# Attention and two gated blocks on one core: the values of two heads as one step, and 1/sum loaded into the output tile

## The chip, the core and the metric

The kernel runs on one core of a Trainium2 chip. The core has TensorE (PE: matmuls and transposes, results to PSUM), VectorE (DVE), ScalarE (ACT), GpSimd (POOL) and SyncE (SP), whose queue starts nearly all DMAs. Each engine works through its own list in order and waits for semaphores of the others. The metric is the device time of one execution in microseconds (us); lower is better.

## The reference, cut to what matters

```
# 4 batches, 8 heads, 576 positions, head width 64
scores = q @ k.T / 8
cum    = cumsum(max(s, 0));  bias = -(cum[:, None] - cum[None, :])
scores = where(causal, -1e9, scores + min(bias, 0))
attn   = exp(scores - max);  attn = attn / (sum(attn) + 1e-9)
x      = attn @ v                          # 4 x 576 x 512 over all heads
# block 1: h = gelu(x @ w_in); u, v = halves of h
#   v = layernorm(v) * g_ln; v_s = w_sg @ v + b_sg; x = x + (u * v_s) @ w_out
# block 2: h = relu(x @ w_in2); the same with its own weights, no g_ln, no residual
```

All operands are float32. Products of the two blocks are taken as three float32r products of high and low parts; those of the attention are plain float32.

## The kernel before, in words

The heads of a batch are taken in pairs; there are 16 pairs, four a batch. For a pair, `transposes` (L604) turns q and k of both heads by TensorE; head 0 then lies on partitions 0 to 63 and head 1 on 64 to 127. `scores(i)` (L620) makes block i of 64 or 128 query rows for both heads, each head on one half of TensorE's rows: a float32 product of q and k (L635), then a float32r product that adds the bias (L638). VectorE adds the mask, takes the row minimum of the negated scores and copies to SBUF (L643), ScalarE takes exp and the row sum (L649). `seg` (L705) turns the exponentials by TensorE in four groups a head (L711) and copies them to SBUF by `copy` (L169). `values` (L717) multiplies them with v for one head: 12 matmuls whose outputs are 64 partitions wide, so each uses half of TensorE's columns. By the table USE the lower half of the columns gets pieces of 768 moving columns and the upper half 896, in one PSUM bank. `finish` (L724) copies the two parts out into the head's 64 partitions of the pair's tile x.

`denominators` (L651) takes the reciprocals of the row sums on VectorE, transposes them and writes them to a scratch tensor in DRAM with four small DMAs; `spread` (L662) reads them back with two DMAs that repeat a row over 64 partitions into a tile rb. When a pair enters the first block, GpSimd multiplies x by rb (L315), and x is split into float32r parts.

A TensorE record of a float32 matmul counts twice in the profile, so a head's 12 value matmuls are 24 records.

What sets the order: every piece of work is a step with a name, a place on a scale of heads and the steps it must follow (`Plan`, L59); `emit` runs through them by place. The places come from tables of numbers (PAIR, HEAD, MOE, WEIGHT and others), and ENG says which engine (A, D, P) does a copy or subtraction in batch 0, in batch 1, later, and in block 2. From the emitted steps a scheduler fixes each engine's list. While the first batch's attention runs, the weights of block 1 are loaded and split (L192 to L198); from then on matmuls of the blocks stand between the attention's steps. After the last pair the rest of block 1 and block 2 follow; the rows of block 2's spatial matrix are loaded, turned by TensorE (L210) and split one after the other through one staging tile.

Six PSUM banks go round among scores, transposes and values; two serve the blocks. SP's queue issues in order, and a DMA whose wait is open holds those behind it.

## Time and profile before

| what | us |
| --- | --- |
| median of 3 runs | 680.57 (677.62 to 680.93) |
| the profiled execution | 679.22 |
| its span, first to last instruction | 677.4 |
| TensorE busy | 659.8 (97%), 4733 matmul records |
| VectorE, ScalarE, GpSimd busy | 374.5, 359.5, 237.4 |
| mean granted TensorE clock | 0.991 |
| share of the chain that ended last | PE 90%, DVE 4%, DMA 3% |

The profile shows one execution. "Busy" counts an instruction from start to end, and for TensorE the end is modelled and reaches beyond the start of the next matmul; so the distance from start to start tells more of what a matmul costs than its duration. A row of the timeline merges neighbours of one line: "x24" is 24 records, and the second number is the time from the first start to the last end.

### The profile page before, as it was taken

The page shows a single profiled execution, that of the slowest core. Times are in us where ns is not written, and L with a number is a line of the kernel's source. Part 1 is how long each engine was busy: PE and PEld are TensorE (multiplying, and loading weights), DVE is VectorE, ACT ScalarE, POOL GpSimd, SP SyncE. Part 2 cuts the span into 40 slices and gives each one's busy share as a digit, 9 for nine tenths or more (in the row PEclk, how much of TensorE's full clock was granted, in tenths as well). Part 3 has the DMA queues.
Part 4 walks back from the last instruction along what each step waited for, and adds up shares of the span by engine and source line. Part 5 has one row for each costly group of instructions (what it writes and reads, how often), then busy time and mean ns, then how long its engine had stood idle before and what let it go on. Part 6 is the DMA issues. An engine that isn't in the chain of part 4 may idle for free.

```text
span 677.4 us, 13008 instructions
## 1 busy us (share of the span) xinstructions
PE 659.8 (97%) x4733; PEld 577.4 (85%) x4733; DVE 374.5 (55%) x1060; ACT 359.5 (53%) x927; POOL 237.4 (35%) x340
## 2 busy tenths in 40 slices
PE   8999999999999999999999999996999999999997
PEld 5877786789888889897888989995998998998996
DVE  7789969953538765547673488556792112111010
ACT  5678788874537664537562355326544426424322
POOL 2125634511621201412311544656594228014121
PEclk9999899999999999999999999999899999999999
DMA  6566663332331441330311433455241000010011
GB/s 156 149 167 196 162 185 105 82 88 55 96 94 26 121 106 25 97 89 8 104 54 36 132 122 87 130 157 176 74 130 49 32 32 19 15 53 11 11 54 47
DMA packets 87193, 59.84 MB, mean 88 GB/s; under 512 B 64469, under 2 KB 72661, under 8 KB 87129
## 3 DMA queue, kind: packets, MB, share of 16 engines
q1 hardware_dynamic: 85928, 58.71, 30.6%
q8 instruction: 37, 0.61, 0.4%
q10 hardware_dynamic: 1200, 0.30, 0.2%
q14 instruction: 28, 0.22, 0.1%
HBM read 44.59 MB, written 14.39 MB: 87 GB/s over the span
## 4 chain that ended last, share of the span: by engine, by line
PE 90%; DVE 4%; DMA 3%; SPq 1%; issue 1%; ACT 0%; POOL 0%
PE acc L721 8%; PE pp L711 8%; PE s L635 6%; PE pm L418 3%; PE pm L420 3%; PE pm L419 3%; PE pb L445 3%; PE pb L444 3%; PE pb L446 3%; PE pm L339 3%; PE pm L444 2%; PE pb L418 2%; PE pb L339 2%; PE pb L340 2%; PE pb L420 2%; PE pb L419 2%
## 5 line engine op out<-in xcount | busy, mean ns | idle before, releaser
L649 ACT ACTIVATE p<-p,mx 128x576 f32<-128x576 f32 (+4 forms) x160 | 88.5, 554 | 27.7 <-DVE mx L643 27.1
L455 POOL TENSOR_TENSOR g<-u,g 128x256 fp32r<-128x256 f32 (+1 forms) x48 | 39.0, 816 | 163.3 <-ACT g L169 124.5
L635 PE MATMUL s<-qk 64*128 64x288 f32 (+4 forms) x384 | 72.0, 411 | 1.2 <-DVE qk L169 0.8
L643 DVE CUSTOM_DVE_ANT_0 p<-s,mask 128x448 f32<-128x448 f32 (+4 forms) x160 | 62.0, 422 | 15.4 <-PE s L638 14.9
L711 PE MATMUL pp<-idf,p 128*128 128x128 f32 x480 | 68.7, 277 | 1.1 <-DVE pt L169 0.9
L721 PE MATMUL acc<-pt,raw_v 128*64 128x64 f32 (+3 forms) x768 | 63.9, 290 | 1.3 <-DVE mx L643 1.3
L711 PEld LDWEIGHTS pp<-idf,p 128*128 128x128 f32 x480 | 53.6, 140 | 9.7 <-issue 1.9
L721 PEld LDWEIGHTS acc<-pt,raw_v 128*64 128x64 f32 x768 | 50.0, 139 | 12.8 <-issue 4.3
L638 PE MATMUL s<-bias,ones 64*64 64x64 f32 (+4 forms) x192 | 57.1, 467 | 0.0
L450 DVE TENSOR_TENSOR u<-u,pm 128x256 f32<-128x256 f32 (+1 forms) x32 | 14.3, 448 | 66.6 <-PE pm L449 66.5
L635 PEld LDWEIGHTS s<-qk 64*128 64x128 f32 (+1 forms) x384 | 36.9, 176 | 14.2 <-issue 6.0
L169 ACT COPY pt<-pp 128x512 f32<-128x512 f32 (+2 forms) x72 | 38.1, 542 | 18.0 <-PE pp L711 17.1
L370 POOL TENSOR_TENSOR sm<-sm,half_pow 128x1 f32<-128x1 f32 (+1 forms) x38 | 27.6, 728 | 45.6 <-DVE sm L369 41.3
L450 DVE TENSOR_TENSOR u<-u,pb 128x320 f32<-128x320 f32 (+1 forms) x32 | 14.6, 455 | 47.4 <-PE pb L449 47.4
L315 POOL TENSOR_TENSOR x<-x,rb 128x576 f32<-128x576 f32 x16 | 23.1, 1442 | 50.3 <-ACT x L169 46.1
L444 PE MATMUL pm<-sgh,vh 128*128 128x256 f32 (+1 forms) x128 | 39.0, 307 | 0.6 <-ACT sgh L216 0.6
L169 ACT CAST g<-u 128x256 fp32r<-128x256 f32 (+1 forms) x40 | 17.0, 434 | 42.1 <-DVE u L450 42.1
L291 POOL TENSOR_TENSOR xl<-x,xh 128x576 fp32r<-128x576 f32 x24 | 34.7, 1461 | 9.8 <-ACT xh L169 7.8
L444 PE MATMUL pb<-sgh,vh 128*128 128x320 f32 (+1 forms) x128 | 38.0, 297 | 0.0
L445 PE MATMUL pb<-sgl,vh 128*128 128x320 f32 (+1 forms) x128 | 38.0, 297 | 0.0
L445 PE MATMUL pm<-sgl,vh 128*128 128x256 f32 (+1 forms) x128 | 37.5, 294 | 0.2 <-DVE sgl L217 0.2
L418 PE MATMUL pm<-xh,inh 128*128 128x256 f32 (+1 forms) x120 | 37.2, 310 | 0.0
(258 smaller groups left out, 1989.0 us busy)
## 6 DMA issues: line engine op xcount, KB each, us to landing
rb<-rec_d SPq DMA_DIRECT2D x32, 144.0 KB
x_d<-x SPq DMA_DIRECT2D x16, 288.0 KB
x<-x_d SPq DMA_DIRECT2D x16, 288.0 KB
raw<-in_q_dram SPq DMA_DIRECT2D x32, 128.0 KB
raw_v<-in_v_dram SPq DMA_DIRECT2D x32, 128.0 KB
stage<-in_moe_w_in_dram SPq DMA_DIRECT2D x8, 512.0 KB
stage<-in_moe_w_in_dram SPq DMA_DIRECT2D x16, 256.0 KB
out_dram<-o SPq DMA_DIRECT2D x16, 256.0 KB
```

The costliest lines, as they stand in the source:

```text
L169: (e.copy if e is nc.scalar else e.tensor_copy)(out_, in_)
L291: engine("xlo", phase).tensor_tensor(xl[:, kk, :S], x, fl(xh[:, kk, :S]), ALU.subtract)
L418: nc.tensor.matmul(pu, W["inh"][:, kk, f], xh[:, kk, c], start=(kk == 0), stop=False)
L444: nc.tensor.matmul(pz, vh[sb][:, f], W["sgh"][:, sb, c], start=(sb == 0), stop=False)
L445: nc.tensor.matmul(pz, vh[sb][:, f], W["sgl"][:, sb, c], start=False, stop=False)
L455: engine("glo", phase).tensor_tensor(gl, u, fl(gh), ALU.subtract)
L635: nc.tensor.matmul(st[a, e][:m, c0:c0 + w], st["qk"][rows, 0, qc], st["qk"][rows, 1, kc], start=True, stop=False)
L638: nc.tensor.matmul(st[a, e][:m, c0:c0 + w], ones[rows, :m], bias[n % 2][rows, kc], start=False, stop=True)
L643: nc.vector.tensor_tensor_reduce(out=pts[g][i][:m, kc], in0=st[a, e][:m, c0:c0 + w], in1=mask[:m, d0:d0 + w], scale=-0.125, scalar=3e38 if ...
L649: nc.scalar.activation(p, p, AF.Exp, bias=mx[g][:m, i:i + 1], scale=-1.0, accum_out=sums[n % 2][:m, NB * e + i:NB * e + i + 1])
L711: nc.tensor.transpose(ps[:, w:w + 128], pt[qb][:, kb * 128:kb * 128 + 128], idr if qb == kb and kb else idf)
L721: nc.tensor.matmul(st["acc"][64 * a:64 * a + 64, a0:a0 + w], raw_v[m % 2][:, kb, odd], st["x"][i][:, c0:c0 + w], start=j in (0, 1), stop=j ...
```

## The change

- `values` is one step for a pair. It takes two PSUM banks; each entry of USE is done for head 0 on the lower half of the columns and straight after for head 1 on the upper half. So the two halves get equal pieces in turn, 1664 columns each, and both heads' turned exponentials are kept until then (a tile for each head and group).
- `spread` puts 1/sum into the pair's tile x itself. `finish` multiplies on VectorE, x = acc * x, in two instructions of 128 partitions (384 and 192 columns). The copies of `finish`, the tile rb and GpSimd's multiplication go. x is now taken at `spread`, which must follow the splitting of x three pairs before; before, `spread` followed the splitting of the pair before.
- Scores: the step S2 makes blocks 0 to 3 and S4 block 4; before, 0 to 2 and 3 to 4.
- Small DMAs: the reciprocals are written with one DMA in place of four, the two rows of bias come with one in place of two (the second part of a row now lies 32 partitions further on).
- Every place in the tables and several engines in ENG are new. Among these: the low part of block 1's input weights goes from GpSimd to VectorE, the normalisation of v in batch 0 from VectorE to GpSimd, the low part of x in batch 1 from GpSimd to VectorE, in block 2 the high part of the gated product from ScalarE to GpSimd.
- The attention's exponentials and a part of block 2's tiles are placed by hand in one stretch of SBUF. Paths that would transpose in float32r are added, but their limits RAW and QKW (32) are never reached by 16 pairs.

```diff
-            if layer == 1:
-                engine("xm", phase).tensor_tensor(x, x, pairs[b * KD + kk]["rb"], ALU.mult)
             split_x(x, st["xh"], st["xl"], kk, phase)
...
-            for e in range(2 if n else 0):
-                nc.sync.dma_start(out=fl(bias[n % 2][D * e:D * e + 2]), in_=cum_d[2 * n + e])
+            if n:
+                nc.sync.dma_start(out=fl(bias[n % 2][::32]), in_=cum_d[2 * n:2 * n + 2].rearrange("h i t -> (h i) t"))
...
-            for i in range(4):
-                nc.sync.dma_start(out=rec_d[n % 4][:, 32 * i:32 * i + 32], in_=rt[32 * i:32 * i + 2 * NB])
+            nc.sync.dma_start(out=rec_d[n % 4].rearrange("c (b i) -> b c i", b=4), in_=rt)
...
         def spread():
-            st["rb"] = rb = ap.tile([128, S], F32, tag="rb", name="rb")
+            x = x_of(b)(j)
             for e in range(2):
                 row = rec_d[n % 4][NB * e:NB * e + NB].rearrange("c p -> (c p)")[64:]
-                nc.sync.dma_start(out=rb[D * e:D * e + D], in_=row.rearrange("(o t) -> o t", o=1).to_broadcast([D, S]))
+                nc.sync.dma_start(out=x[D * e:D * e + D], in_=row.rearrange("(o t) -> o t", o=1).to_broadcast([D, S]))
...
-        plan.add(f"B{n}", t0 + head["B"], spread, [f"R{n}", f"sp1.{(n - 1) // KD}.{(n - 1) % KD}"])
+        plan.add(f"B{n}", t0 + head["B"], spread, [f"R{n}", f"sp1.{(n - XB) // KD}.{(n - XB) % KD}" if n >= XB else None])
...
         def values():
-            st["acc"] = psa.tile([128, 512], F32, tag="a", name="acc")
+            acc = pair["acc"] = [psa.tile([128, 512], F32, tag="a", name="acc") for i in range(2)]
 
             for j, (i, c0, w, kb, a, a0) in enumerate(USE):
-                nc.tensor.matmul(st["acc"][64 * a:64 * a + 64, a0:a0 + w], raw_v[m % 2][:, kb, odd], st["x"][i][:, c0:c0 + w],
-                                 start=j in (0, 1), stop=j in (9, 11))
+                for e in range(2):
+                    nc.tensor.matmul(acc[a][D * e:D * e + D, a0:a0 + w], raw_v[m % 2][:, kb, e], pair["x", e, i][:, c0:c0 + w],
+                                     start=j in (0, 1), stop=j in (9, 11))
 
         def finish():
-            x = x_t(h // 2)
-            copy("fc", phase, x[rows, :384], st["acc"][0:64, :384])
-            copy("fd", phase, x[rows, 384:], st["acc"][64:128, :192])
+            x, acc = x_t(h // 2), pair["acc"]
+            for a, c in enumerate((slice(0, 384), slice(384, S))):
+                nc.vector.tensor_tensor(x[:, c], acc[a][:, :c.stop - c.start], x[:, c], ALU.mult)
...
-WEIGHT = {"wv": (3.54, 0.99), "wu": (6.51, 1.82), "sg": (3.14, 5.74), "wo": (4.59, 6.75), "ahead": 0.88}
+WEIGHT = {"wv": (-0.99, 0.33), "wu": (6.32, 1.86), "sg": (2.65, 7.0), "wo": (-3.21, 6.28), "ahead": 3.45}
```

How the lists move at three places that the prediction speaks of. First TensorE's list of the kernel before, around the values of a late head (pp is a group of turned exponentials, pm a product of the blocks):

```order
1919 L711 MATMUL pp<-idf,p_1_147 128x128
1920 L711 MATMUL pp<-idf,p_2_149 128x128
1921 L721 MATMUL acc<-pt,raw_v_121 64x320 [waits DVE_49]
1922 L721 MATMUL acc<-pt,raw_v_121 64x192 x3
1923 L721 MATMUL acc<-pt,raw_v_121 64x64 x3
1924 L721 MATMUL acc<-pt,raw_v_121 64x192
1925 L721 MATMUL acc<-pt,raw_v_121 64x64 x2
1926 L721 MATMUL acc<-pt,raw_v_121 64x128
1927 L721 MATMUL acc<-pt,raw_v_121 64x64 [waits DMAHW7_49]
1928 L711 MATMUL pp<-idf,p_2_149 128x128 [waits DVE_49]
1929 L711 MATMUL pp<-idf,p_3_151 128x128 x2
1930 L711 MATMUL pp<-idf,p_4_153 128x128
```

TensorE's list of the changed kernel around the values of a pair:

```order
1431 L456 MATMUL pm<-r_212,s_115 128x256
1432 L748 MATMUL acc<-pt,raw_v_124 64x320 [waits DVE_49]
1433 L748 MATMUL acc<-pt,raw_v_124 64x320
1434 L748 MATMUL acc<-pt,raw_v_124 64x192 [waits DVE_49]
1435 L748 MATMUL acc<-pt,raw_v_124 64x192 x5
1436 L748 MATMUL acc<-pt,raw_v_124 64x64 x6
1437 L748 MATMUL acc<-pt,raw_v_124 64x192 x2
1438 L748 MATMUL acc<-pt,raw_v_124 64x64 x4
1439 L748 MATMUL acc<-pt,raw_v_124 64x128
1440 L748 MATMUL acc<-pt,raw_v_124 64x128 [waits DVE_49]
1441 L748 MATMUL acc<-pt,raw_v_124 64x64 x2
1442 L737 MATMUL pp<-idf,p_0_127 128x128 [waits Activation_49]
```

The 24 matmuls of a pair now stand together. Over the whole list the values stand in 47 unbroken pieces before and in 22 now, the scores in 44 before and 32 now, and TensorE turns into or out of a piece of values or scores 182 times before and 107 times now. Up to the first score of pair 7 these counts are 71 and 40 turns, and 22 and 9 pieces of values; up to there the changed list also has 48 block products of 256 columns and 13 transposes more.

Second, VectorE's list of the changed kernel at the finish of pair 7 (L754; xl is the low part of x, rows L301). Before there was no such place on VectorE in this batch: ScalarE copied, and GpSimd multiplied later:

```order
398 L179 COPY pt<-pp 128x384 [waits PE_49]
399 L301 TENSOR_TENSOR xl<-x,xh 128x576 [waits Pool_49]
400 L179 COPY pt<-pp 128x512 [waits PE_49]
401 L179 COPY pt<-pp 128x192 [waits PE_49]
402 L301 TENSOR_TENSOR xl<-x,xh 128x576 [waits Pool_49]
403 L475 TENSOR_TENSOR xr<-xr,pm 128x256 [waits DMAHW5_49,PE_49]
404 L475 TENSOR_TENSOR xr<-xr,pm 128x256 [waits DMAHW1_49,DMAHW2_49,DVE_49,PE_49]
405 L179 COPY pt<-pp 128x384 [waits PE_49]
406 L754 TENSOR_TENSOR x<-acc,x 128x384 [waits DMAHW3_49,DMAHW4_49,DMAHW0_49,DVE_49]
407 L754 TENSOR_TENSOR x<-acc,x 128x192
408 L301 TENSOR_TENSOR xl<-x,xh 128x576 [waits Pool_49]
409 L179 COPY qk<-pst 128x512 [waits PE_49]
```

Row 406 names DMAs and VectorE itself but not TensorE; so do the finishes of pairs 11 and 15, while the other 13 name TensorE too. Behind it stand the copies of the next pair's q and k.

Third, SP's list at the start, of the kernel before:

```order
1 L157 DMA sr<-in_s_dram 32x576
2 L588 DMA raw<-in_q_dram 128x4x64 x2
3 L589 DMA raw<-in_q_dram 64x2x64
4 L588 DMA raw_v_121<-in_v_dram 128x4x64
5 L588 DMA raw_v_121<-in_v_dram 128x4x64 [waits DMAHW0_49]
```

and of the changed one:

```order
1 L167 DMA sr<-in_s_dram 32x576
2 L194 DMA stage<-in_moe_w_out_dram 128x1024
3 L592 DMA raw<-in_q_dram 128x4x64 x2
4 L593 DMA raw<-in_q_dram 64x2x64
5 L194 DMA stage<-in_moe_w_in_dram 128x1024 [waits DMAHW0_49,DVE_49]
```

A 512 KB load of weights now stands ahead of the first q, a second behind it, and a third ahead of the second pair's q.

## Rows read from the trace of the kernel before

**Rows 1.** Windows: engines' busy time, start of pair 7 at 124.1 (clock, DMA last)
```profile
0.00:124.10 124.10, 117.78 (x900) 89.89 (x900) 102.46 (x313) 92.99 (x259) 46.86 (x81) 0.99 0.59 156
124.10:372.20 248.10, 248.10 (x2015) 217.24 (x2015) 148.32 (x481) 141.46 (x375) 59.30 (x74) 1.00 0.26 72
372.20:458.00 85.80, 85.29 (x568) 81.23 (x567) 57.10 (x125) 35.48 (x80) 44.83 (x64) 1.00 0.41 124
458.00:478.00 20.00, 13.75 (x67) 11.19 (x66) 14.54 (x37) 10.97 (x32) 11.85 (x20) 0.83 0.54 157
478.00:677.40 199.40, 194.87 (x1190) 177.88 (x1189) 52.11 (x106) 78.59 (x184) 74.54 (x105) 1.00 0.14 44
```

**Rows 2.** Windows of L721 (values) alone: PE, then weight loads
```profile
0.00:124.10 124.10, 26.66 (x288) 19.73 (x288) 0.99 0.59 156
124.10:372.20 248.10, 37.27 (x480) 30.30 (x480) 1.00 0.26 72
```

**Rows 3.** Timeline of PE around one whole head (start, length, line, what, records)
```profile
158.04 0.82 PE L711 MATMUL pp<-idf,p 128*128 128x128 f32 x6
158.70 1.04 PE L610 MATMUL pst<-idf,raw 128*128 128x128 f32 x8
...
163.12 0.71 PE L711 MATMUL pp<-idf,p 128*128 128x128 f32 x5
163.76 1.79 PE L721 MATMUL acc<-pt,raw_v 128*64 128x320 f32 x24
165.49 0.33 PE L711 MATMUL pp<-idf,p 128*128 128x128 f32 x1
```

**Rows 4.** Timeline of PE, values cut in pieces
```profile
55.10 0.75 PE L721 MATMUL acc<-pt,raw_v 128*64 128x320 f32 x2
55.78 0.77 PE L711 MATMUL pp<-idf,p 128*128 128x128 f32 x5
...
352.64 1.31 PE L721 MATMUL acc<-pt,raw_v 128*64 128x192 f32 x20
353.88 0.41 PE L418 MATMUL pm<-xh,inh 128*128 128x320 f32 x1
```

**Rows 5.** Timeline of PE, from block products into scores
```profile
174.90 0.28 PE L466 MATMUL pm<-g,outl 128*128 128x256 f32 x1
175.02 0.28 PE L464 MATMUL pm<-g,outh 128*128 128x256 f32 x1
175.23 1.55 PE L635 MATMUL s<-qk 64*128 64x448 f32 x7
```

**Rows 6.** Timeline of PE, spatial weights of block 2 (idle before, releaser, in brackets)
```profile
463.68 0.63 PE L210 MATMUL pb<-idf,stage 128*128 128x128 f32 x4 [1.68 <-DMA stage<-in_moe_w_spatial_dram]
...
468.38 0.66 PE L210 MATMUL pb<-idf,stage 128*128 128x128 f32 x4 [1.19 <-DMA stage<-in_moe_w_spatial_dram]
...
472.43 1.09 PE L210 MATMUL pb<-idf,stage 128*128 128x128 f32 x4 [2.57 <-DMA stage<-in_moe_w_spatial_dram]
...
474.81 0.63 PE L339 MATMUL pb<-inh,xh 128*128 128x512 f32 x1
...
478.31 0.39 PE L339 MATMUL pb<-inh,xh 128*128 128x512 f32 x1
```

**Rows 7.** Lines by form, DVE and POOL (busy, mean ns, idle before and releaser)
```profile
L169 DVE COPY x<-acc 64x384 f32<-64x384 f32 x24 | 13.1, 545 | 9.1 <-PE acc L721 8.2 <-POOL xl L291 0.7
L450 DVE TENSOR_TENSOR u<-u,pb 128x320 f32<-128x320 f32 x18 | 8.7, 483 | 28.2 <-PE pb L449 28.2
L315 POOL TENSOR_TENSOR x<-x,rb 128x576 f32<-128x576 f32 x16 | 23.1, 1442 | 50.3 <-ACT x L169 46.1 <-DMA rb<-rec_d 4.1
L397 DVE TENSOR_TENSOR vl<-g,vh 128x512 fp32r<-128x512 f32 x8 | 6.1, 756 | 6.8 <-ACT vh L169 6.7
```

**Rows 8.** Timeline of SP's queue, first reciprocals out and back
```profile
18.77 2.14 SPq L660 DMA_DIRECT2D rec_d<-rt  x4
22.44 1.12 SPq L666 DMA_DIRECT2D rb<-rec_d  x2
```

More of the change, by code (lines that the diff above doesn't have):

```diff
@@ L41 @@
[L41 to L52 removed]
+PA, PM, XB, RAW, LOW, QKW = 6, 2, 3, 32, 0, 32
@@ L391, in vc @@
                 if tb == NT:
-                    rest["v"] = w2p.tile([128, S + REM], F32R, tag="stg2", name="rest_v")[:, :DF]
                     v_parts(g[0:64], vh[NT], s14[0:64])
@@ L498, in keep @@
         def keep():
-            if first:
-                rest["g"] = w2p.tile([128, 8 * 128], F32R, tag="rest", name="rest").rearrange("p (i t) -> p i t", i=8)
             copy("rg", phase, rest["g"][:, :, 64 * (b % 2):64 * (b % 2) + 64], fl(st["g8"][:, :, 256:320]))
@@ L559, in attention_two_moe_kernel @@
         nc.gpsimd.memset(t, 1.0)
-    rec_d = [dr.tile([2 * NB, 128], F32, name=f"rec_d{i}") for i in range(4)]
+    rec_d = [dr.tile([32, 128], F32, name=f"rec_d{i}") for i in range(4)]
     ones = ap.tile([128, 128], F32R, name="ones")
@@ L566, in attention_two_moe_kernel @@
     for e in range(2):
-        nc.vector.memset(fl(ones[D * e:D * e + 2]), 1.0)
+        for i in range(2):
+            nc.vector.memset(fl(ones[D * e + 32 * i:D * e + 32 * i + 1]), 1.0)
     def cumulate():
@@ L594, in plan_pair, with fetch @@
         phase = min(b, 2)
+        words, qk_words = 2 * n >= RAW, int(2 * n >= QKW)
+        def fetch(r, queue=nc.sync):
+            r = r.rearrange("p (t e d) -> p t e d", t=2 * NT + 1, e=2)
+            for i, src in enumerate((q, k)):
+                load(r[:, NT * i:NT * i + NT], src, b, j, r[REM * i:REM * i + REM, 2 * NT], queue if i else nc.sync)
         def ldqk():
-            st["raw"] = ap.tile([128, (2 * NT + 1) * 2 * D], F32, tag="raw", name="raw")
-            r = st["raw"].rearrange("p (t e d) -> p t e d", t=2 * NT + 1, e=2)
-            for i, src in enumerate((q, k)):
-                load(r[:, NT * i:NT * i + NT], src, b, j, r[REM * i:REM * i + REM, 2 * NT], nc.scalar if n == 0 and i else nc.sync)
+            if qk_words:
+                nc.sync.dma_start(out=fl(raws[1]), in_=qk_d[n])
+            else:
+                fetch(raws[0], nc.sync if n else nc.scalar)
         def transposes():
-            raw = st["raw"]
+            raw, ident, like = raws[qk_words], idq if qk_words else idf, F32R if qk_words else F32
             c, cr = slice(0, NT * 128), slice(NT * 128, S)
@@ L708, in seg @@
             for qb, kb in SEG[i]:
-                nc.tensor.transpose(ps[:, w:w + 128], pt[qb][:, kb * 128:kb * 128 + 128],
-                                    idr if qb == kb and kb else idf)
+                pt, ident, turned, like = ((ptr[n % 3][qb], idq, idqr, F32R) if n >= RAW and qb >= LOW else
+                                           (pts[n % 3][qb], idf, idr, F32))
+                nc.tensor.transpose(ps[:, w:w + 128].bitcast(like), pt[:, kb * 128:kb * 128 + 128],
+                                    turned if qb == kb and kb else ident)
@@ L730, in plan_head @@
         step("X1", lambda: seg(1), [f"S4.{m}", f"X0.{n}", f"X1.{n - 1}"])
-        step("X2", lambda: seg(2), [f"X1.{n}", f"V3.{n - 1}"])
+        step("X2", lambda: seg(2), [f"X1.{n}"])
         step("X3", lambda: seg(3), [f"X2.{n}"])
-        step("V3", values, [f"X3.{n}", f"ldv{m}", f"V3.{n - 1}"])
-        step("F1", finish, [f"V3.{n}", f"F1.{n - 1}"] + x_free)
+        if odd:
+            where = HEAD0 if n < H else HEAD
+            plan.add(f"V3.{m}", n + where["V3"], values, [f"X3.{n - 1}", f"X3.{n}", f"ldv{m}"])
+            plan.add(f"F1.{m}", n + where["F1"], finish, [f"V3.{m}", f"F1.{m - 1}", f"B{m}"])
```

117 lines of the change are left out of this document (69 added, 48 removed).

## The prediction

> **What bounds the kernel now.** I read the windows first, cut at the first score of pair 7, at the end of the values, and around block 2's spatial weights; then the values alone, then TensorE's timeline at a few places.
>
> From 124.1 to 372.2 TensorE has no idle time at all, while VectorE is busy for 148.3 of 248.1 and ScalarE for 141.5 [rows 1]. What TensorE saves there is saved in the end, unless another engine makes it wait. From 478.0 on it is nearly as full, and the change does not touch its matmuls there. Up to 124.1 the picture is mixed: TensorE 117.8, VectorE 102.5, ScalarE 93.0 of 124.1, with DMA at 0.59 [rows 1]; TensorE's busy time is flattered by modelled ends, so this stretch is set by chains over three engines. From 458 to 478 TensorE is busy for only 13.75 of 20 [rows 1].
>
> **The values.** A whole head takes 1.73 from its first start to the next instruction's [rows 3]. A transpose inside a run takes 0.66 / 6 = 0.11, so the 0.64 before the values is five of them and 0.09 for turning from full width to half columns [rows 3]. Into scores the distance is 0.21 where it was 0.12 between block products, again 0.09 [rows 5]. I use 0.09 for every turn into or out of values and scores. That leaves 1.64 for a head's matmuls, in which the upper columns work off 896 moving columns and the lower only 768.
>
> After the change a pair brings 1664 columns to each half, in equal pieces. Scaled by the longer half, a pair takes 1.64 x 1664 / 896 = 3.05 in place of 3.28. After 124.1 there are 20 heads in 25 pieces (480 records, 37.27 busy [rows 2]). Each piece's busy time reaches 0.06 past the next start (1.79 against 1.73), so the pieces really take 37.27 - 25 x 0.06 = 35.8. Afterwards: 10 x 3.05 + 13 pieces x 0.09 = 31.7. Gain 4.1.
>
> Bounds. The rest of a cut head, 20 records with 704 columns on its longer half, takes 353.88 - 352.64 - 0.09 = 1.15, or 1.63 ns a column [rows 4]; by that a pair takes 2.72 and the gain is 35.8 - 28.4 = 7.4. If the halves only share one rate and balance gives nothing, a pair takes 3.28, and only fewer ends are saved: 35.8 - 34.0 = 1.8. I take 4.1, since it comes from the whole head, which is what the new step is made of.
>
> Here a rule speaks against the change. A cut piece of one 320-column matmul takes 0.68 - 0.09 = 0.59, with the other half empty [rows 4], so 1664 columns one after the other would take 3.07: the old step already runs at 1.87 times one half's speed. The Trainium skill's page "TensorE: Matmul & The Clock Gate", section on packing small matmuls, measures 2.38 times for three column tiles, 0.79 a tile; carried over to two tiles, my estimate is 1.6 times, which would leave nothing for balance. The trace is past that already, so I count it as a rival with a small chance: the lower bound 1.8, and the sum would be 2.3 less.
>
> **The turns.** After pair 7's start the lists show 111 turns before and 67 now; 12 of the 44 that go are ends of values, counted above. 32 x 0.09 = 2.9. It could be 0 where a turn hides under a wait, but TensorE has no idle time there [rows 1], and 4 if all 44 count.
>
> **Spatial weights of block 2.** Each load into the single staging tile can start only when TensorE has turned the one before; TensorE waits 1.68 + 1.19 + 2.57 = 5.4 for them [rows 6]. The clock then falls: a 512-column product shows 0.63 at 474.8 and 0.39 at 478.3 [rows 6], and the granted clock is 0.83 over these 20 us [rows 1], a third of them at the 1.2 GHz level, 3.4 lost at most, part of it while waiting anyway. I count 2.4. In the new list 48 residual products, then 36 of block 2's first product, then 13 and 12 products with a few others stand between one turn and the next. From load to load the old list takes 468.38 - 463.68 = 4.7 and 4.05 [rows 6]; the first two gaps are now 7 to 9 us and cover it, the last two about 3.7 to 3.9 and leave 0.5 to 1 each. So 1.5 of waiting stays and the clock holds: gain 5.4 - 1.5 + 2.4 = 6.3; bounds 0, if the load is late for another reason, and 8.8.
>
> **The first 124 us.** TensorE's own need falls: values from 26.66 - 22 x 0.06 = 25.3 [rows 2] to 6 x 3.05 + 9 x 0.09 = 19.1, and 31 turns go, 13 of them ends of values, so 18 x 0.09 = 1.6. Together 7.8. Into the room comes work from later, 48 block products at 0.12 [rows 5] and 13 transposes at 0.11, 7.2. If TensorE set the pace, pair 7 would begin at the same 124 and 7.2 would be missing later. VectorE hardly gets lighter up to there: 8 copies at 0.545 go [rows 7], with them 6 normalising steps and 4 casts, but 8 subtractions of 128x512 come, at 0.756 by the nearest row, and 12 multiplications; a 320-column multiplication from PSUM takes 0.483 [rows 7], so 384 and 192 columns are near 0.9 a pair. I put this at +1 us. The start is worse: 512 KB now stand ahead of the first q, at 156 GB/s [rows 1] 3.3 us, and some 1.2 MB more than before ahead of pair 1's, 8 us, though pair 0's turned exponentials and weight splitting can fill a part. I take a net gain of 4; bounds -4 (all 8 and 3.3 lost) and 10.
>
> **What costs nothing.** The copies out of the values leave ScalarE and the multiplication (23.1 us [rows 7]) leaves GpSimd; neither bounds. Fewer small DMAs: the four writes took 2.14 us of SP's queue for a pair, the two reads 1.12 [rows 8]; about 1.6 a pair is saved there, 26 in all, but TensorE never waited for these. It only brings 1/sum earlier. VectorE gets some 15 us more in the middle stretch (multiplications, subtractions); at 148 of 248 it has room, and if the cover fails it shows as waits for scores.
>
> **A wait is added.** finish now needs 1/sum on VectorE, with two of six PSUM banks held. Behind it stand the copies of the next groups and then the reductions of the scores, and TensorE waits for those. In the new list the values of a pair come after the scores of the next pair, some 20 us after its own, and the old round trip took 22.44 - 18.77 = 3.7 from writing to reading back [rows 8]. In 13 of 16 pairs the values come last; at pairs 7, 11 and 15 the DMA does. I count nothing.
>
> **Sum.** 4.1 + 2.9 + 6.3 + 4 = 17.3. The profiled execution took 679.2, 1.35 below the median of 680.57 and inside the three runs' spread. 679.2 - 17.3 = 662.
>
> **The rivals.**
> - Two halves at one rate (the rule above): values gain 1.8 in the middle and about 1 less at the start: 665.5. For it: nothing but the page; against: 1.87 already. 0.12.
> - The start slips and VectorE sets the first stretch: 4 becomes -4, 670. For it: VectorE's 102.5 of 124.1 and the loads ahead of q; against: TensorE was often what others waited for. 0.18.
> - The spatial loads stay late because SP's queue holds them behind other waits: 0 for 6.3, 668. For it: in-order issue; against: the first gaps of 7 to 9 us. 0.1.
> - Slower: finish waits for 1/sum. The place is VectorE's row of finish, worst where x comes free late. GpSimd once waited 4.1 for rb [rows 7]. If in each of the 12 pairs after the first batch VectorE stands for the round trip of 3.7 and the four free banks cover 1.7 of it, 12 x 2 = 24: 686. It decides from 17.3 / 12 = 1.4 a pair. For it: three finishes where the DMA is last; against: the 20 us ahead in the others. 0.08.
>
> **How the numbers follow.** My forecast has 0.52. The forecast's own bounds and the first three rivals lie from 649 to 675; below that needs every upper bound at once. About 0.5% (3.4 us) is what a measurement can tell from no change. Faster 0.88: the forecast and the three milder rivals, less a little for several of them together. Within 0.5%: 0.05, the milder ones added up. Slower: 0.07, nearly all of the last rival.
>
> **What would show it.** Right: values in at most 22 pieces, a whole pair near 3.1 from start to start; pair 7's first score near 124 with more block products before it; no wait of more than 1 us at the spatial transposes and a clock near 1.0 there; TensorE without idle time from there to the end of the values. Wrong: a pair's values at 3.4; a first score of pair 7 past 130; VectorE's finish idle on a DMA, with TensorE's transposes or scores waiting behind for copies.

## The result, and the profile after

The changed kernel takes 669.44 us (median of 4 runs, 667.86 to 669.82), the kernel before 680.63 in the same measurement; the ratio is 0.984, interval 0.981 to 0.987. The forecast was 662 with a range of 649 to 675: faster, as said, but by 11.2 us in place of 17.3. The profiled execution took 669.26, its span is 667.5.

The windows of the changed kernel, cut at the same events as [rows 1]: first score of pair 7 (now at 138.6), end of the values (363.8), 20 us around block 2's spatial weights, and the rest. Columns: window, length, busy time (records) of PE, PEld, DVE, ACT, POOL, then granted clock, DMA share, GB/s.

```profile
0.00:138.60 138.60, 124.06 (x962) 95.44 (x962) 102.70 (x329) 94.68 (x257) 47.33 (x90) 0.94 0.56 145
138.60:363.80 225.20, 225.17 (x1927) 197.66 (x1927) 153.31 (x493) 114.67 (x313) 35.77 (x56) 1.00 0.29 77
363.80:450.00 86.20, 84.42 (x577) 80.41 (x576) 56.87 (x129) 40.96 (x93) 36.54 (x46) 1.00 0.44 128
450.00:470.00 20.00, 18.91 (x105) 15.54 (x104) 15.18 (x37) 12.82 (x38) 10.04 (x20) 1.00 0.46 133
470.00:667.50 197.50, 192.51 (x1171) 175.75 (x1169) 55.04 (x122) 64.43 (x148) 75.16 (x122) 0.99 0.14 45
```

Two opposite things are to be seen. From pair 7's first score to the end it is 667.5 - 138.6 = 528.9 us, before it was 677.4 - 124.1 = 553.3: 24.4 less, of which 7.2 is work that now lies ahead of pair 7. So 17.2 are gained there, where the forecast had 4.1 + 2.9 + 6.3 = 13.3. Up to pair 7 it takes 14.5 us longer; 7.2 of that is the moved work, so 7.3 are lost where the forecast had a gain of 4. TensorE's own account of the 14.5: it is idle for 138.60 - 124.06 = 14.5 in place of 6.3 [rows 1], 8.2 more, and its mean granted clock up to pair 7 is 0.94 in place of 0.99, at most 0.06 x 138.6 - 0.01 x 124.1 = 7.1 more; its need at full clock would be about the same (forecast: 7.8 saved, 7.2 moved in).

The values alone, for the first two of these windows (to compare with [rows 2]), and the timeline of TensorE around two whole pairs (start, length, line, what, records):

```profile
0.00:138.60 138.60, 20.85 (x288) 16.59 (x288) 0.94 0.56 145
138.60:363.80 225.20, 31.35 (x480) 25.58 (x480) 1.00 0.29 77
```
```profile
244.34 2.98 PE L748 MATMUL acc<-pt,raw_v 128*64 128x320 f32 x48
247.25 1.64 PE L737 MATMUL pp<-idf,p 128*128 128x128 f32 x13
...
268.06 2.98 PE L748 MATMUL acc<-pt,raw_v 128*64 128x320 f32 x48
270.96 0.77 PE L737 MATMUL pp<-idf,p 128*128 128x128 f32 x5
```

A pair takes 2.91 and 2.90 from its start to the next instruction's; a single head took 1.73 [rows 3]. One count of columns has to be put right here: by the kernel's table USE, and by the records of the trace, a head has 768 moving columns on the lower half and 832 on the upper, not 896; a pair so brings 1600 columns to each half, not 1664.

The spatial weights of block 2, the same rows as [rows 6] (idle time before and its releaser in brackets):

```profile
447.96 0.65 PE L220 MATMUL pb<-idf,stg 128*128 128x128 f32 x4
...
456.89 0.60 PE L220 MATMUL pb<-idf,stg 128*128 128x128 f32 x4
...
461.55 0.66 PE L220 MATMUL pb<-idf,stg 128*128 128x128 f32 x4 [0.63 <-DMA stg<-in_moe_w_spatial_dram]
...
466.30 0.46 PE L220 MATMUL pb<-idf,stg 64*128 64x64 f32 x4
```

Waits of 5.4 have become 0.63 and 0.47 (the second at the fifth transpose of that row block), and the clock in these 20 us is 1.00 where it was 0.83.

Where the first stretch loses its time is seen in the starts of each pair's first score (from the timelines of TensorE; "other" counts TensorE's records in between that are neither scores, values nor transposes for the attention):

| from first score of | before, us | other | after, us | other |
| --- | --- | --- | --- | --- |
| start to pair 1 | 16.9 | | 26.3 | |
| pair 1 to pair 4 | 44.0 | 15 | 52.7 | 20 |
| pair 4 to pair 7 | 63.2 | 66 | 59.6 | 109 |

The first two lines lose 9.4 and 8.7; in the third the changed kernel does 43 records more in 3.6 us less. The start, in TensorE's timeline of the changed kernel, and four windows behind it:

```profile
1.17 4.88 PE L145 MATMUL idle<-first 128*128 128x512 bf16 x11 [1.17 <-DVE first L140]
8.10 1.06 PE L621 MATMUL pst<-idf,raw 128*128 128x128 f32 x8 [2.05 <-DMA raw<-in_q_dram]
...
10.04 2.38 PE L660 MATMUL s<-qk 64*64 64x64 f32 x12 [0.77 <-DVE qk L179]
```
```profile
10.00:12.50 2.50, 2.46 (x16) 1.90 (x17) 0.09 (x1) 0.00 (x0) 0.00 (x0) 0.51 1.10 274
...
17.50:20.00 2.50, 2.50 (x9) 1.73 (x6) 1.52 (x5) 1.74 (x6) 0.00 (x0) 0.50 0.16 36
...
22.50:25.00 2.50, 2.50 (x19) 2.50 (x19) 2.23 (x5) 2.50 (x6) 1.81 (x3) 0.76 0.57 129
25.00:27.50 2.50, 2.50 (x25) 2.16 (x24) 1.92 (x5) 1.69 (x5) 1.36 (x2) 1.00 0.50 110
```

TensorE waits 2.05 for q, which stands behind 512 KB of w_out, and 0.77 for a copy; behind these waits the granted clock is 0.50, the 1.2 GHz level, from 10 until about 23. Pair 0's scores and transposes take 16.3 us where they took 8.7. Then VectorE fills up; windows 30 to 60 of the kernel before and of the changed one:

```profile
30.00:40.00 10.00, 10.00 (x87) 8.06 (x85) 7.41 (x32) 8.24 (x28) 3.06 (x3) 1.00 0.56 153
40.00:50.00 10.00, 10.00 (x88) 8.20 (x87) 8.22 (x26) 7.01 (x22) 3.44 (x3) 1.00 0.64 161
50.00:60.00 10.00, 9.31 (x87) 7.18 (x86) 8.99 (x28) 9.02 (x23) 4.20 (x5) 1.00 0.66 183
```
```profile
30.00:40.00 10.00, 8.00 (x77) 5.81 (x76) 10.00 (x29) 6.43 (x16) 3.03 (x4) 1.00 0.58 159
40.00:50.00 10.00, 8.72 (x66) 6.54 (x64) 9.85 (x35) 7.01 (x21) 4.17 (x4) 1.00 0.77 221
50.00:60.00 10.00, 9.53 (x101) 8.00 (x102) 9.80 (x27) 8.20 (x23) 3.44 (x4) 1.00 0.75 176
```

Before, TensorE was full here and VectorE had room; now VectorE is full (29.65 of 30) and TensorE is idle for 3.75. The waits of TensorE, and those of VectorE for finish (us in total, times, longest):

```profile
PE pm L220 <- DMA stage<-in_moe_w_sg_dram: 2.3, 1, 2.3
PE pst L621 <- DMA raw<-in_q_dram: 2.0, 1, 2.0
PE pst L621 <- ACT pt L179: 1.6, 1, 1.6
PE pp L737 <- DVE mx L668: 1.5, 1, 1.5
...
PE pp L737 <- DVE x L754: 0.9, 3, 0.5
```
```profile
DVE x L754 <- DMA x<-rec_d: 4.8, 3, 2.6
...
DVE x L754 <- PE acc L748: 4.3, 4, 1.5
```

VectorE's finish does wait for 1/sum, 4.8 us in all, but only 0.9 of TensorE's waiting is put down to finish. The rival of a slower kernel did not come.

### The profile page after: what moved, and what is told of

The parts are those of the page before. It is cut to its first block, busy times and chain, and to the rows that moved or that the text cites. A ratio compares the mean times of both kernels' runs of the same rounds, so it can differ in the third digit from the quotient of the medians.

```text
span 667.5 us, 12894 instructions
## 1 busy us (share of the span) xinstructions
PE 645.1 (97%) x4733; PEld 564.8 (85%) x4733; DVE 383.1 (57%) x1109; ACT 327.6 (49%) x846; POOL 204.8 (31%) x332
## 4 chain that ended last, share of the span: by engine, by line
PE 81%; DVE 7%; DMA 6%; issue 2%; ACT 2%; SPq 1%; POOL 1%; DVEq 0%; POOLq 0%; ACTq 0%
PE pp L737 7%; PE s L660 7%; PE acc L748 6%; PE pm L347 3%; PE pm L425 3%; PE pm L348 3%; PE pm L427 3%; PE pm L426 2%; PE pm L451 2%; PE pb L453 2%; PE pb L452 2%; PE pb L451 2%; PE pm L453 2%; PE pm L452 2%; PE pb L427 2%
## 5 line engine op out<-in xcount | busy, mean ns | idle before, releaser
L668 DVE CUSTOM_DVE_ANT_0 p<-s,mask 64x64 f32<-64x64 f32 (+4 forms) x160 | 61.5, 422 | 13.1 <-PE s L663 12.6
L663 PE MATMUL s<-bias,ones 64*128 64x288 f32 (+3 forms) x192 | 53.8, 488 | 0.0
L748 PE MATMUL acc<-pt,raw_v 128*64 128x64 f32 (+3 forms) x768 | 52.2, 287 | 0.2
L748 PEld LDWEIGHTS acc<-pt,raw_v 128*64 128x64 f32 x768 | 42.2, 140 | 11.1 <-issue 2.5
L301 POOL TENSOR_TENSOR xl<-x,xh 128x576 fp32r<-128x576 f32 x20 | 28.8, 1457 | 69.2 <-ACT xh L179 69.0
L179 POOL CAST g<-u 128x256 fp32r<-128x256 f32 (+1 forms) x40 | 17.2, 441 | 106.6 <-DVE u L457 77.8
L179 DVE COPY pt<-pp 128x512 f32<-128x512 f32 (+1 forms) x72 | 37.2, 530 | 12.4 <-PE pp L737 11.8
L179 ACT COPY pt<-pp 128x512 f32<-128x512 f32 (+2 forms) x56 | 28.7, 532 | 31.1 <-PE pp L737 31.1
L497 ACT COPY o<-pb 128x512 f32<-128x512 f32 x13 | 7.5, 589 | 57.1 <-PE pb L495 55.1
L425 PE MATMUL pm<-xh,inh 128*128 128x320 f32 (+1 forms) x112 | 35.4, 316 | 0.0
L374 POOL TENSOR_SCALAR sm<-sm 128x1 f32<-128x1 f32 (+1 forms) x33 | 7.9, 240 | 87.7 <-DVE g L297 73.5
```

What stands on the lines that cost most here:

```text
L179: (e.copy if e is nc.scalar else e.tensor_copy)(out_, in_)
L301: engine("xlo", phase).tensor_tensor(xl[:, kk, :S], x, fl(xh[:, kk, :S]), ALU.subtract)
L425: nc.tensor.matmul(pu, W["inh"][:, kk, f], xh[:, kk, c], start=(kk == 0), stop=False)
L663: nc.tensor.matmul(st[a, e][:m, c0:c0 + w], ones[rows, :m], bias[n % 2][rows, kc], start=False, stop=True)
L668: nc.vector.tensor_tensor_reduce(out=pts[g][i][:m, kc], in0=st[a, e][:m, c0:c0 + w], in1=mask[:m, d0:d0 + w], scale=-0.125, scalar=3e38 if ...
L748: nc.tensor.matmul(acc[a][D * e:D * e + D, a0:a0 + w], raw_v[m % 2][:, kb, e], pair["x", e, i][:, c0:c0 + w], start=j in (0, 1), stop=j in ...
```

## The experiments

The question was the first stretch: forecast +4, found -7.3. Twelve kernels were run. "Pair 1", "pair 7" and "pair 8" are the starts of these pairs' first scores in the profiled execution; up to pair 7 all changed kernels have the same 140 TensorE records outside the attention (warm_longer has 7 warm-up products more), while up to pair 8 weights_as_before, bias_first and no_loads_good_start have 24 block products more than the others, worth 24 x 0.12 = 2.9. The ratio is taken to the kernel before in the same measurement (681.02 for the four rows from q_first, 678.80 from bias_first on, 679.98 from loads_gone on, 680.07 for the last), so compare rows by it. These starts are of one execution each, and executions of one kernel differ by several us.

| kernel | median | ratio to before (interval) | pair 1 | pair 7 | pair 8 |
| --- | --- | --- | --- | --- | --- |
| before | 680.63 | | 16.9 | 124.1 | 145.3 |
| changed | 669.44 | 0.984 (0.981 to 0.987) | 26.3 | 138.6 | 157.2 |
| q_first | 670.71 | 0.984 (0.980 to 0.988) | 28.3 | 141.2 | 159.8 |
| warm_longer | 665.91 | 0.979 (0.974 to 0.984) | 25.8 | 137.0 | 155.6 |
| weights_as_before | 670.51 | 0.985 (0.982 to 0.989) | 18.5 | 138.9 | 161.1 |
| values_by_head | 698.32 | 1.025 (1.022 to 1.029) | 25.4 | 143.0 | 164.1 |
| bias_first | 671.83 | 0.990 (0.987 to 0.994) | 23.3 | 140.2 | 162.5 |
| pair1_first | 667.38 | 0.982 (0.979 to 0.986) | 19.4 | 139.5 | 158.1 |
| spatial_as_before | 682.80 | 1.005 (1.002 to 1.008) | 26.6 | 139.8 | 158.4 |
| halves_unequal | 668.92 | 0.984 (0.981 to 0.988) | 25.3 | 132.9 | 151.7 |
| loads_gone | 667.48 | 0.983 (0.981 to 0.986) | 25.4 | 136.0 | 154.6 |
| before_loads_gone | 684.93 | 1.005 (1.003 to 1.008) | 19.4 | 127.0 | 146.2 |
| low_on_gpsimd | 667.68 | 0.983 (0.981 to 0.985) | 27.5 | 138.8 | 157.4 |
| no_loads_good_start | 663.79 | 0.978 (0.974 to 0.982) | 18.8 | 132.7 | 154.9 |

**q_first.**
```diff
-        plan.add(f"ldqk{n}", t0 + where["ldqk"], ldqk, [f"cp{n}", f"T{n - 1}"])
+        plan.add(f"ldqk{n}", t0 + where["ldqk"] - (20 if n == 0 else 0), ldqk, [f"cp{n}", f"T{n - 1}"])
```


> Edit: in the changed kernel the first pair's q is loaded ahead of the 512 KB of w_out instead of behind it; apart from a few neighbouring rows nothing moves. Theory (the first stretch lost its time at the start, where TensorE waits 2.05 us for q after its warm-up products and then runs at the 1.2 GHz level until about 20): the gap goes, the granted clock of the first 30 us is near that of the kernel before, pair 0's first score stands near 8.2 (10.0 in the changed kernel), pair 1's near 18 to 20 (26.3), pair 7's near 132 (138.6), and the time falls by 5 to 8 us to 661-664. Rival (the loads ahead of pair 1 and the splitting of weights on VectorE hold pair 1 back anyway): only the start moves, by some 2 us, pair 1 stays at 24 to 26, and the time is 667-669.

The gap before q is gone and pair 0's first score stands at 8.4, but the time is no better. The next wait took its place, the bias rows behind the same weights (TensorE's timeline):

```profile
8.40 1.34 PE L660 MATMUL s<-qk 64*64 64x64 f32 x12 [1.18 <-DVE qk L179]
13.06 1.11 PE L663 MATMUL s<-bias,ones 64*64 64x64 f32 x6 [3.32 <-DMA bias<-ch]
```

The clock fell as before (0.77 over the first 30 us in both). Both theories missed: pair 1 came later, not earlier.

**warm_longer.**
```diff
-MORE = {..., "w0": 11, ...}
+MORE = {..., "w0": 18, ...}
```


> Edit: 18 warm-up products instead of 11 on TensorE, about 3.1 us more at 0.44 us each, which cover the 2.05 us gap before q arrives; every load stays where the changed kernel has it. Theory that the clock alone costs it: pair 0's first score stays near 10, its scores take near 6 us instead of 10.7, pair 1's first score comes near 20 to 21 (26.3), the time falls by 4 to 6 us to 664-665. Rival (loads and splitting): pair 1 stays at 24 to 26 although the clock is up; time 668-670.

TensorE comes from the warm-up to q with little idle time, pair 0's first score stands at 9.3 with the clock up, and then waits 1.25 for the bias rows: by 12.5 the clock is down again, and pair 1 comes only 0.5 earlier. So this trace doesn't show a start with the clock up. The median lies near the expected time, but its interval overlaps that of the changed kernel. The six executions range from 663.0 to 672.5, and the time goes with the granted clock of the whole execution: 663.0 to 664.2 at 0.995 and 0.996, 667.6 to 672.5 at 0.979 to 0.989. The profiled one (667.6, 0.989) is of the second kind. This speaks for a price of the lower clock of some 5 us, without showing where in the kernel it is paid.

**weights_as_before.**
```diff
-WEIGHT = {"wv": (-0.99, 0.33), "wu": (6.32, 1.86), "sg": (2.65, 7.0), "wo": (-3.21, 6.28), "ahead": 3.45}
+WEIGHT = {"wv": (3.54, 0.99), "wu": (6.51, 1.82), "sg": (3.14, 5.74), "wo": (4.59, 6.75), "ahead": 0.88}
```


> Edit: the table of places for block 1's weights (loads and splitting) is that of the kernel before; all else as changed. Theory (the weights' places cost the first stretch 7 us more than the moved work explains): pair 1's first score near 18, pair 7's near 131, and the time falls by 5 to 8 us to 661-664. Rival C of the prediction (VectorE and the attention's steps set the first stretch, whatever the weights): pair 1 comes back to 18, but pair 7 stays at 136 to 139 and the time at 667-670, since VectorE is as full as before.

The start is healed: clock 1.00 over the first 30 us, pair 1 at 18.5. Yet pair 7 is at 138.9 and the time at 670.5. My theory failed; the times expected of rival C (the second rival of the prediction) came out to within 0.5 us. But its mechanism did not, as the windows from 30 to 100 show:

```profile
30.00:60.00 30.00, 25.76 (x202) 20.02 (x202) 23.43 (x78) 20.09 (x60) 6.44 (x8) 0.89 0.54 142
60.00:100.00 40.00, 33.56 (x269) 26.65 (x266) 32.87 (x98) 26.68 (x75) 12.59 (x15) 0.87 0.72 179
```

VectorE is not "as full as before": 23.43 of 30, where the changed kernel has 29.65. The chain of waits up to 139 now has 11.4% in loads of w_in and 6.6% in loads of w_sg: what no longer hinders the start comes late. And the lower clock has only moved: up to pair 7 the mean granted clock is 0.94, as in the changed kernel, and TensorE is idle for 17.4 in place of 14.5.

**bias_first and pair1_first.** The first loads of the weights are issued behind the bias rows (cum_d), or behind pair 1's q and k too:
```diff
+            def load_it(name=name, new=new, fetch=fetch, behind=layer == 1 and not before):
+                held[name] = new()
+                with tc.issue_after(last[-1].ins) if behind else nullcontext():
+                    fetch(held[name])
...
```


> Edit: the first loads of block 1's weights are issued on SP's queue behind the first pair's q and behind the bias rows (cum_d), instead of ahead of q; later loads keep their places. With q alone put first (q_first) TensorE waited 3.32 us for the bias rows behind the weights and the clock fell all the same. Theory: any of these waits at the start lets the clock fall to the 1.2 GHz level, and a start without them holds it: granted clock near 1.00 up to 30 us as in weights_as_before, pair 1's first score at 18 to 20, and as nothing else is moved, pair 7's near 131 to 133 and the time 661-665. Rival: the first 140 us are set by the chain of block 1's weights (load into the one staging tile, split on VectorE, next load), so pair 1 comes at 18 to 20 but pair 7 stays at 137 to 140, as in weights_as_before, and the time at 667-671.

> Edit: as bias_first, and the first weight loads stand behind pair 1's q and k as well, so they start some 3 us later still. Theory (the start decides): pair 1 is no earlier than in bias_first by more than 1 us, time within 2 us of bias_first. Rival (the chain of weights decides): the later the weights, the later pair 7: pair 7's first score 2 to 4 us behind bias_first's, time 2 to 4 us more.

In bias_first pair 1's k stands behind the weights (a wait of 2.9), pair 1 comes at 23.3; in pair1_first it comes at 19.4 and the clock is 1.00 over the first 30 us. In both, pair 7 stays at 140. So the theory that the start alone decides is refuted: moving pair 1 by 9 us moves neither pair 7 nor, beyond the intervals, the end. The rival was right on bias_first's pair 7 (not on its pair 1) and wrong on pair1_first: its later weights did not make pair 7 later. But pair1_first, too, is no kernel without the lower clock, which falls from 30 on (0.95 over the stretch up to pair 7):

```profile
30.00:60.00 30.00, 25.40 (x204) 19.40 (x201) 26.45 (x75) 19.06 (x56) 9.34 (x11) 0.93 0.70 194
60.00:100.00 40.00, 33.28 (x265) 28.11 (x263) 29.95 (x87) 24.81 (x68) 9.58 (x13) 0.88 0.53 153
```

**loads_gone and before_loads_gone.**
```diff
-        nc.sync.dma_start(out=st[:, 0:2 * n].bitcast(I32), in_=src.bitcast(I32))
+        if n < DF:
+            nc.sync.dma_start(out=st[:, 0:2 * n].bitcast(I32), in_=src.bitcast(I32))
...
+            raw = g_b.bitcast(I32).rearrange("p (n t) -> p n t", t=2)
...
```


> Left out: the 12 loads of 512 KB of block 1's w_in and w_out; every splitting step stays, but reads a tile of 256 KB that is loaded once at the start, so block 1 computes with other weights. Five starts have now given pair 1's first score anywhere from 18.5 to 28.3 and pair 7's always at 137 to 141. Theory W (the first stretch of the changed kernel is set by the weights' chain: load into a staging tile, 4 to 6.6 us each on the chain of waits, split, next load): without the loads pair 7's first score comes at 128 to 132 and the time falls by 6 to 10 us to 659-663. Rival V (VectorE's order sets it: 103 us busy of 138.6, with the splits, the copies and the scores' reductions in one list): the loads only filled time in which VectorE had other work; pair 7 at 135 to 139, time 666-669.

> Left out: the same 12 loads, in the kernel before. Theory W: there TensorE was idle for 6.3 of its first 124.1 us and loads stood on the chain for few us, so the kernel before gains less than the changed one: pair 7's first score at 120 to 123, time 675-679 (2 to 5 us less). Had both kernels the same cost from the loads (then they explain nothing of the missed gain): 8 to 10 us less, 670-672.

Without the 12 loads the changed kernel's pair 7 starts 2.6 earlier and its median is 2 us lower, within the intervals. The kernel before gains nothing, its median is 4.9 above that of the kernel before in the same measurement, outside both expectations. Its q now stands behind the 256 KB: pair 1 comes 2.5 later; pair 7 comes at 127.0, with 12 block products more ahead of it (1.4). Its twelve executions range from 678.5 to 686.2, and the profiled one took 679.1, so its trace does not show what made most of them longer. Theory W, that the loads alone set the first stretch, falls; alone they cost 2 to 3 us.

**low_on_gpsimd.**
```diff
-ENG = {..., "wlo": "DPPP", ...}
+ENG = {..., "wlo": "PPPP", ...}
```


> Edit: one letter of ENG; the low parts of block 1's w_in (8 subtractions of 128x512, 0.6 to 0.7 us each on VectorE in the changed kernel) go back to GpSimd, where they stood before and take about twice as long. Rival V (VectorE sets the first stretch): 8 x 0.65 = 5 us less for VectorE, time falls by 3 to 5 us to 664-666. Theory W (the chain of the weights): each split takes longer on the chain, time unchanged or up to 4 us more, 669-673.

VectorE loses 8 subtractions of 0.76, GpSimd gets them at 1.33. Pair 7 doesn't move (138.8), the time is 1.8 lower with overlapping intervals. So these eight subtractions are not, alone, what holds pair 7 back. Whether VectorE's fullness does is not settled: from 30 to 60 it is still busy for 28.5 of 30, and the clock up to pair 7 was lower in this execution (0.91 in place of 0.94).

**no_loads_good_start.** loads_gone, with the one 256 KB load behind the first two pairs' q and k:
```diff
+    def load_g():
+        with tc.issue_after(mark[0].ins):
+            nc.sync.dma_start(out=g_b, in_=moe_g_ln.rearrange("(o d) -> o d", o=1).to_broadcast([128, DF]))
...
```


> Left out: the loads of block 1's weights, as in loads_gone; and the one 256 KB tile that stands for them is loaded behind the first two pairs' q and k, so that neither q nor the bias rows have a large load ahead of them (in loads_gone TensorE still waited 1.1 us for q and ran at the lower clock to about 25). So far the start alone (pair1_first: pair 1 at 19.4, pair 7 at 139.5) and the loads alone (loads_gone: 25.4 and 136.0) each left pair 7 where it was. Theory T, a trade: either the attention starts late or the weights come late, and each alone is enough to hold pair 7 back: with both gone pair 1 comes at 18 to 20, pair 7 at 127 to 131, the time at 658-662. Rival O: what is left is the order of the attention's own steps in the first batch (scores, values of two heads, copies), which takes 18 to 19 us a pair whatever the weights do: pair 7 at 134 to 138 with an early pair 1 too, the time at 664-668.

Pair 1 comes at 18.8 and pair 7 at 132.7, 5.9 before the changed kernel's, with the same work ahead of it. (Pair 8 stands at 154.9, as in loads_gone, but with 24 block products more ahead of it.) The median is 663.8, the lowest of all, 5.6 below the changed kernel; the two intervals still overlap by 0.001. Both marks lie between theory T and rival O: with neither loads nor a late start 5.6 of the 7.3 us come back, and each pair still takes 16 to 24 us from there on. The lower clock is not gone here either (0.96 up to pair 7).

**values_by_head.**
```diff
-            for j, (i, c0, w, kb, a, a0) in enumerate(USE):
-                for e in range(2):
+            for e in range(2):
+                for j, (i, c0, w, kb, a, a0) in enumerate(USE):
```


> Edit: the values of a pair are issued head by head, 12 matmuls for the lower half of the columns and then 12 for the upper half, instead of in turn. The same matmuls, only their order differs. Theory (the two column halves run side by side only while pieces for both stand in turn; one half alone takes 0.59 us for 320 columns, 1.84 ns a column): a pair takes up to 2 x 1664 x 1.84 ns = 6.1 us instead of 2.9, less what overlaps at the change of heads; 16 pairs give +45 to +51 us, 714-720. Rival (both halves share one rate, so order doesn't matter and the gain of the step came from fewer turns alone): a pair stays near 2.9 to 3.0 and the time within 1% of 669.

```profile
173.80 5.44 PE L748 MATMUL acc<-pt,raw_v 128*64 128x320 f32 x48
179.17 0.77 PE L737 MATMUL pp<-idf,p 128*128 128x128 f32 x5
```

The same matmuls in another order take 5.37 a pair in place of 2.91: the two halves of the columns run side by side only while pieces for both stand in turn. The rival of one shared rate is refuted; the theory's 6.1 a pair and 714 to 720 were too high. The time rises by 29, less than 16 x 2.46 = 39, and the markers show where the rest is: from pair 7 to the end it is 552.5 in place of 528.9, 23.6 for ten pairs (24.6 expected), but pair 7's start moves only from 138.6 to 143.0, though six pairs bring 14.8 us more of TensorE's time. That is the clearest row of the study on the first stretch: some 10 us of TensorE's work there cost nothing, and the medians say the same (28.9 more, of which the ten later pairs account for 24.6). TensorE's idle time up to pair 7 is 10.4 in place of 14.5: part of the added work filled gaps.

**halves_unequal.**
```diff
+            for e in range(2):
+                for j, (i, c0, w, kb, a, a0) in enumerate(USE):
+                    nc.tensor.matmul(acc[e][D * a:D * a + D, a0:a0 + w], raw_v[m % 2][:, kb, e], pair["x", e, i][:, c0:c0 + w],
```


> Edit: the values stay one step for a pair, but each head goes to both column halves again, 896 columns on one half and 768 on the other, head 0 into one bank and head 1 into the other; finish takes four instructions of 192 columns instead of two, and multiplies the parts by 1/sum in the wrong places. Theory (the halves run side by side, each at its own pace, so the longer one sets the time): a pair takes 3.2 to 3.3 us instead of 2.93, 16 pairs 4 to 6 us, time 673-676. Rival (both halves share one rate): a pair stays at 2.9 to 3.0, time 669-671.

```profile
239.40 3.22 PE L748 MATMUL acc<-pt,raw_v 128*64 128x320 f32 x48
242.55 1.64 PE L737 MATMUL pp<-idf,p 128*128 128x128 f32 x13
```

A pair takes 3.15 where the changed kernel takes 2.91, so equal pieces in turn are worth 0.24 a pair; two heads apart took 2 x 1.73 = 3.46 [rows 3], so joining them in one piece is worth 0.31, of which 0.09 is one turn. The forecast for balance, 3.28 - 3.05 = 0.23, agrees by luck: with 832 and 1600 columns its sum gives 1.64 x 1600 / 832 = 3.15 in place of 3.05, and 0.13. The longer half's columns do not explain the rest; that pieces of unequal width stand in turn may, which no run separates. In the total nothing is seen: after pair 7 it is 529.9 against 528.9, and the first stretch of this execution happened to be 5.7 shorter, which no step of the edit explains; its six runs spread from 664.6 to 670.4, and the profiled one is the shortest. So one execution's pair 7 can move by as much as most of the differences in the table.

**spatial_as_before.**
```diff
-WEIGHT2 = {"wv": (-0.12, 5.87), "wu": (10.83, 13.19), "sg": (10.11, 10.44), "wo": (3.64, 1.59), "ahead": 4.44}
+WEIGHT2 = {"wv": (-0.17, 10.7), "wu": (11.01, 8.53), "sg": (14.19, 10.73), "wo": (-2.14, 3.37), "ahead": 4.88}
```


> Edit: the table of places for block 2's weights is that of the kernel before, so its spatial rows are turned by TensorE with 13, 21, 29 and 13 lines of the list between them instead of 47, 37, 16 and 18. Theory (TensorE waits for these loads, 5.4 us in the kernel before, and then runs at the lower clock): waits of 1 to 2.6 us come back at the two or three short gaps, the granted clock there falls below 0.95, and the time rises by 4 to 8 us to 673-677. Rival D of the prediction turned round (where the rows stand decides nothing, the loads are late or early for another reason): waits as in the changed kernel, 1.1 us together, time 668-671.

The old places cost 13.4 us by the medians, 14 by the ratios: the whole gain of the change and more, and more than the 4 to 8 expected. Windows of this kernel, and of the changed one:

```profile
440.00:460.00 20.00, 17.05 (x86) 14.99 (x85) 12.80 (x28) 6.17 (x15) 9.41 (x13) 0.91 0.54 168
460.00:480.00 20.00, 15.10 (x80) 11.77 (x79) 16.72 (x40) 12.95 (x36) 11.21 (x20) 0.88 0.39 115
480.00:500.00 20.00, 18.90 (x120) 18.23 (x120) 15.57 (x35) 8.96 (x23) 12.24 (x22) 0.78 0.31 101
```
```profile
440.00:460.00 20.00, 19.41 (x105) 16.34 (x104) 13.19 (x31) 8.85 (x25) 8.54 (x14) 1.00 0.69 207
460.00:480.00 20.00, 18.50 (x131) 16.59 (x130) 18.18 (x44) 13.13 (x34) 10.08 (x17) 1.00 0.24 71
480.00:500.00 20.00, 20.00 (x127) 18.98 (x126) 12.53 (x29) 7.32 (x17) 17.35 (x24) 1.00 0.42 126
```

TensorE's idle time grows by 6.9 here and the clock falls to 0.78; its waits for the spatial rows are 2.3 of that, for the high part of a gated product 2.3, for split input weights 1.9. Rival D (the prediction's third) is refuted. The table moves all of block 2's weights, so the run prices it as a whole, not the spatial rows alone.

## Why the prediction was right, and what in it was wrong

- **Values**: right in the mechanism, with a wrong count of columns. 4.1 was forecast for the ten pairs of the middle stretch; with 0.06 taken off each of 13 pieces it is now 31.35 - 0.8 = 30.6 against 35.8, so 5.2. With the columns of the table, 832 and 1600, the forecast's own sum would have given 10 x 3.15 + 1.2 = 32.7 and a gain of 3.1. A pair takes 2.91 - 0.09 = 2.82 and not 3.15: scaling a head by its longer half undersized the term, since it does not count what equal pieces in turn save (halves_unequal). The bound from the cut head was the nearer row: with 640 columns on its longer half, not 704, it gives 1.15 / 640 = 1.80 ns a column and 2.87 a pair. The rival of one rate for both halves is refuted. Its "1.87 already" does not hold: by the rate of values_by_head, 5.37 / 3200 = 1.68 ns a column, the old step ran at 1600 x 1.68 / 1.64 = 1.6 times one half's speed; the new one runs at 5.37 / 2.91 = 1.85. The Trainium skill's "TensorE: Matmul & The Clock Gate", section "Measured speedup vs the span model", gives 2.38 times for three column tiles. Carried over to two tiles (1.6, my estimate) that is where the old order stood, and equal pieces in turn went past it.
- **Turns**: 2.9 forecast, not measured by itself. From pair 7 to the end of the values it is 248.1 - 225.2 = 22.9 less; 7.2 of that lie earlier now and 28 records or so (1853 against 1825) after the values, at least 28 x 0.12 = 3.4. The 12 left are 5.2 for the values and some 7 more, where 2.9 were forecast. Summed from each TensorE record's start to the next, the 324 records of scores in this stretch take 37.0 in place of 40.4, and the turned exponentials 104 ns each in place of 115, which is 3.0 over their 272 records. So the 7 lies about half in the scores, which stand in fewer pieces, and half in these transposes, which less often lead into values or scores. How much of it is turns of 0.09 stays open.
- **Spatial weights**: right in mechanism. Waits of 1.1 were left where 1.5 were forecast, and the clock held; the gaps between row blocks are 8.9, 8.9, 4.7 and 4.8. From the end of the values to the end of the span it is 303.7 after 305.2 with the 28 records more, so about 5, where 6.3 were forecast. spatial_as_before gives no price of this term, since it moves all of block 2's weights in a list they were not placed for.
- **The first 124 us**: wrong, and beyond the bound of -4: -7.3. The prediction's own sign of being wrong, a first score of pair 7 past 130, came (138.6). Two things in the step failed. It counted 7.8 us of TensorE's saved time as room for other work, as if TensorE set the pace; what it saved came back as idle time (14.5 in place of 6.3), and values_by_head shows the same from the other side, where some 10 of 14.8 us of TensorE's time cost nothing. And of the 3.3 and 8 us of loads at the start it charged no more than 7.8 - 1 - 4 = 2.8, taking the rest as hidden, where pair 1 came 9.4 later: behind the waits for q and a copy the clock stood at the 1.2 GHz level for some 13 us, which I had not foreseen, and the next three pairs lost 8.7 more. The second rival, "the start slips and VectorE sets the first stretch", had 670, and the time is 669.4. Its first half is what happened. Its second half is seen in the windows 30 to 60 of the changed kernel, but in weights_as_before VectorE was less full there and pair 7 no earlier, and low_on_gpsimd does not settle it. That its total fits is luck in part: it had -4 and 13.3, measured were -7.3 and 17.2.
- **Finish**: cost nothing, as counted; it was read from the waits and not tried by a run of its own.

So the time is 669.4 because the terms after pair 7 gave 17.2 and not 13.3, and the first stretch took 7.3 and did not give 4: 17.2 - 7.3 = 9.9, the difference of the spans. The direction was right for the reasons given; that the total came no further from 662 owes 3.9 us to terms that were sized too small.

What stays open is what sets the first stretch now. It is not the start alone (six kernels with pair 1 from 18.5 to 28.3 have pair 7 at 137 to 141), not the loads alone, not the eight subtractions alone, and not TensorE's own work. Loads and start together are worth about 5.6 of the 7.3 us. One rival was not tried: the lower clock. In every changed kernel the mean granted clock up to pair 7 is between 0.89 and 0.96, in the kernel before it is 0.99; where the start was healed the clock fell later, so no run shows this stretch without it, and it can be the result of the waits as well as a cause of the delay. The other thing common to all of these kernels is the new order of the attention's steps in the first batch. Between pairs 1 and 4 TensorE has 7.6 us of named waits, 0.6 before: 2.9 for reductions of scores, 2.0 for copies of turned groups and of q and k, 0.5 for finish, and 2.3 for a load of w_sg. That order was not tried by itself.

## What to carry to other kernels

A saving on an engine is worth its price only in stretches where that engine is full by its distances from start to start; where three are as near to full as here (95, 83 and 75% of the first stretch before), count first what the slack swallows. Where several chains are nearly equally long, taking one away moves little: test them together before calling one the cause. A granted clock that is back at 1.00 in one window says nothing of the next ones: read it over the whole stretch. And the starts of single executions move by several us; a difference of that size needs the medians.

## What was not expected of the hardware

- After waits of 2.05 and 0.77 the granted clock was 0.50 from 10 to about 23 us, although TensorE had records running in nearly all of that time, the scores of pair 0; it rose while transposes of 128x128 ran. After a single wait of 1.48 at the same place (weights_as_before), and after 0.44 and 1.50 in pair1_first, it stayed at 1.00. The Trainium skill's page "TensorE: Matmul & The Clock Gate", section "HAM oscillation — how this bites in real kernels", describes a kernel whose TensorE waits for DMA between its groups of matmuls and starts the next group at the lower clock each time. The trace agrees in that the clock was at 0.50 behind a wait of 2.05 for DMA; the second wait here, 0.77, was for VectorE's copy.
- Column halves pay for order: the same 24 matmuls took 2.91 us in turn and 5.37 us half after half.
